# Both matrix products of a token pair by seven block products, in units of 42 matmuls

## The chip, the core and the metric

The kernel runs on one core of a Trainium2 chip. Its time is the device time of one execution, in microseconds (us). Before the change the median of three executions is 830.62 us (828.80 to 830.89).

## The reference

Attention with a sliding window of 64 positions feeds an MLP mixer: a product over tokens, then one over channels. There are 8 batches of 576 tokens, so 4608 tokens of 512 channels. All is float32. The part that the change touches is the last two lines, the channel products with 1536 hidden units:

```python
attn_out = _attn_ref(q, k, v)                    # softmax over a window of 64
x = attn_out.transpose(0, 2, 1, 3).reshape(B, S, H * D)
xt = x.transpose(0, 2, 1)
h = np.maximum(xt @ w_tok1, 0.0) @ w_tok2
u = x + h.transpose(0, 2, 1)
h2 = np.maximum(u @ w_ch1, 0.0) @ w_ch2
return u + h2
```

## The kernel before

Every float32 operand of a product is held as a high part and a low part (type float32r), and a product is three matmuls: high x high, low x high, high x low. A function `split` makes the two parts: ScalarE copies the high part (L101), another engine subtracts it from the source for the low part (L104). For hidden values `relu_split` does it with a rectifier on ScalarE (L614) and one VectorE instruction for the low part (L615).

The first 324 us compute attention and the token products and store `u` to DRAM as nine chunks of 512 tokens; they overlap with the channel products of chunk 0. Then come the channel products of chunks 1 to 8. All tiles are 128 partitions x 512 columns; the 1536 hidden units are 12 tiles, the 512 channels are 4.

*Plain chunks (0, 1, 2).* `gemm1` adds 12 matmuls into a PSUM bank for each of 12 hidden tiles, and `gemm2` makes 4 output tiles out of the 12 hidden ones, half of them at a time in chunks 1 and 2. Beside chunk 1, `weight_steps` forms sums of the blocks of `w_ch1` in float32, splits them and stores them to DRAM (`w1s`), three hidden tiles wide (384 columns), one step for each hidden tile; `quarters` are the blocks of weights that need no sum and are stored whole at the end of chunk 0.

*Pairs (chunks 3+4, 5+6, 7+8).* Two chunks of tokens and two halves of channels and of hidden units make a product of 2 x 2 blocks. `pair_f` does the first product for a hidden block `f` (6 per pair) by seven block products of 6 matmuls each, in the order of `PRODUCTS`. They go into four PSUM banks P, Q, R, S, and three products accumulate on top of an earlier one. Sums of the banks are made by VectorE in SBUF tiles `x1`, `x2`, `x3` (L853 to L865), and each of the four block results goes through `relu_split`. Its operands are combinations of the inputs (`sums`, `sum4`, `prep`), made for a whole pair beforehand by VectorE and ScalarE. After every two hidden blocks, 8 output tiles are made by plain `gemm2` calls of 12 matmuls each, with all of `w_ch2` in SBUF (`w2hi`, `w2lo`), and `add_out` (L645) adds each to the running sum `uf`.

*Order.* Each engine executes its instructions in the order of the program text; SyncE (SP) issues the loads and stores from one queue. `load_w1` fetches the block weights of a hidden block into one of three slots of the old `w1` buffers, three blocks ahead. Eight PSUM banks alternate between a hidden block and the next (`BANKS`).

## Time and profile before

| | before |
|---|---|
| median of 3 executions | 830.62 us (828.80 to 830.89) |
| span of the profiled execution | 827.4 us |
| instructions | 15250 |
| TensorE (PE) busy | 814.4 us, 98%, 5860 matmuls |
| VectorE (DVE) busy | 511.1 us, 62% |
| ScalarE (ACT) busy | 336.6 us, 41% |
| GpSimd (POOL) busy | 106.5 us, 13% |
| DMA moved | 136.51 MB, mean 165 GB/s |

The profiled execution has no time of its own beside its span; the span is 3.2 us below the median of the runs, and that distance is carried along. The page gives an average over stages of very different kinds: 324 us of attention and token products, two plain chunks, three pairs. It is read by cutting the span into these stages, and in each of them by looking for the engine that never waits. An engine's matmul rate can be read from the chain of waits, where a run of matmuls without a wait between them stands as one row. The core's 16 DMA engines share the loads and stores; SPq is the queue that SP issues to.

### The profile page before, as it was taken

The page shows a single profiled execution, that of the slowest core. Times are in us where ns is not written, and L with a number is a line of the kernel's source. Part 1 is how long each engine was busy: PE and PEld are TensorE (multiplying, and loading weights), DVE is VectorE, ACT ScalarE, POOL GpSimd, SP SyncE. Part 2 cuts the span into 40 slices and gives each one's busy share as a digit, 9 for nine tenths or more (in the row PEclk, how much of TensorE's full clock was granted, in tenths as well). Part 3 has the DMA queues.
Part 4 walks back from the last instruction along what each step waited for, and adds up shares of the span by engine and source line. Part 5 has one row for each costly group of instructions (what it writes and reads, how often), then busy time and mean ns, then how long its engine had stood idle before and what let it go on. Part 6 is the DMA issues. An engine that isn't in the chain of part 4 may idle for free.

```text
span 827.4 us, 15250 instructions
## 1 busy us (share of the span) xinstructions
PE 814.4 (98%) x5860; PEld 676.9 (82%) x5860; DVE 511.1 (62%) x1365; ACT 336.6 (41%) x1014; POOL 106.5 (13%) x117
## 2 busy tenths in 40 slices
PE   8989999999999999999999999999999999999998
PEld 6758888888889878888888888878888878888886
DVE  5987899799773993773444535277625277525352
ACT  6988989888864530331221202032202033202020
POOL 3632534444330000000000000000000000000000
PEclk9999999999999999999999999999999999999999
DMA  9847778777645629634506443334433234432002
GB/s 354 284 148 243 237 243 291 231 228 276 193 132 174 193 65 273 185 96 136 182 1 237 143 180 111 118 111 171 170 159 135 95 131 167 176 137 90 1 1 101
DMA packets 69672, 136.51 MB, mean 165 GB/s; under 512 B 7008, under 2 KB 39264, under 8 KB 67680
## 3 DMA queue, kind: packets, MB, share of 16 engines
q1 hardware_dynamic: 67488, 133.71, 47.4%
q10 hardware_dynamic: 2112, 1.84, 0.7%
q8 instruction: 46, 0.75, 0.4%
q14 instruction: 26, 0.21, 0.1%
HBM read 104.66 MB, written 30.87 MB: 164 GB/s over the span
## 4 chain that ended last, share of the span: by engine, by line
PE 84%; DVE 8%; ACT 4%; issue 2%; DMA 1%; POOL 0%; POOLq 0%; DVEq 0%; SPq 0%; ACTq 0%
PE gp L847 19%; PE op L635 11%; PE gp L627 8%; PE h L364 5%; PE up L412 5%; PE op_4a L635 4%; PE op_2b L635 4%; PE op_2a L635 4%; PE op_0b L635 4%; PE op_0a L635 4%; PE op_4b L635 4%; PE xp L316 4%; PE s L274 3%; PE pp L304 3%; PE up L405 2%; ACT e L297 2%
## 5 line engine op out<-in xcount | busy, mean ns | idle before, releaser
L847 PE MATMUL gp<-m,w1hi 128*128 128x512 f32 x504 | 155.3, 390 | 0.7 <-DVE x L855 0.7
L297 ACT ACTIVATE e<-e,nm 128x128 f32<-128x128 f32 x288 | 112.2, 397 | 6.5 <-DVE nm L289 6.3
L847 PEld LDWEIGHTS gp<-m,w1hi 128*128 128x128 f32 x504 | 94.5, 188 | 21.0 <-DVE x L855 1.5
L847 PE MATMUL gp<-m,w1lo 128*128 128x512 f32 x252 | 98.0, 389 | 0.0
L614 ACT ACTIVATE ghi<-x 128x512 fp32r<-128x512 f32 x54 | 34.1, 632 | 119.9 <-DVE x L857 68.3
L289 DVE CUSTOM_DVE_ANT_0 e<-s,mask 128x128 f32<-128x128 f32 x288 | 65.3, 285 | 10.6 <-PE s L274 10.5
L851 ACT COPY x<-gp 128x512 f32<-128x512 f32 x18 | 10.4, 578 | 143.3 <-PE gp L847 143.3
L615 DVE SCALAR_TENSOR_TENSOR glo<-x,ghi 128x512 fp32r<-128x512 f32 x54 | 37.4, 692 | 38.1 <-ACT ghi L614 38.1
L614 ACT ACTIVATE ghi<-gp 128x512 fp32r<-128x512 f32 x50 | 29.9, 597 | 70.0 <-PE gp L627 70.0
L627 PE MATMUL gp<-uhi,w1lo 128*128 128x512 f32 x144 | 56.0, 389 | 0.0
L627 PE MATMUL gp<-ulo,w1hi 128*128 128x512 f32 x144 | 56.0, 389 | 0.0
L627 PE MATMUL gp<-uhi,w1hi 128*128 128x512 f32 x144 | 56.0, 389 | 0.0
L297 ACT ACTIVATION_READ_ACCUMULATOR e<-e,nm 128x1 f32 x288 | 55.9, 194 | 0.0
L847 PEld LDWEIGHTS gp<-m,w1lo 128*128 128x128 f32 x252 | 47.3, 188 | 9.9
L615 DVE SCALAR_TENSOR_TENSOR glo<-gp,ghi 128x512 fp32r<-128x512 f32 x50 | 34.4, 688 | 25.4 <-ACT ghi L614 25.3
L635 PE MATMUL op<-glo,w2hi 128*128 128x512 f32 x128 | 49.8, 389 | 0.0
L635 PE MATMUL op<-ghi,w2hi 128*128 128x512 f32 x128 | 49.8, 389 | 0.0
L635 PE MATMUL op<-ghi,w2lo 128*128 128x512 f32 x128 | 49.8, 389 | 0.0
L316 PEld LDWEIGHTS xp<-v,pt 128*64 128x64 f32 x1152 | 36.6, 138 | 12.9 <-ACT e L297 9.4
L104 POOL TENSOR_TENSOR xlo<-x,xhi 128x512 fp32r<-128x512 f32 x32 | 41.6, 1300 | 43.6 <-ACT xhi L101 42.9
L304 PE MATMUL pp<-ident,e 128*128 128x128 f32 x288 | 45.4, 282 | 1.5
L274 PE MATMUL s<-k,q 64*64 64x128 f32 x1152 | 41.8, 277 | 2.6 <-DMA k<-kh 0.9
(161 smaller groups left out, 1827.9 us busy)
## 6 DMA issues: line engine op xcount, KB each, us to landing
v<-vh SPq DMA_DIRECT2D x36, 512.0 KB, 4.4
w1hi<-w1s SPq DMA_DIRECT2D x18, 896.0 KB, 4.7
w1lo<-w1s SPq DMA_DIRECT2D x18, 896.0 KB, 6.5
raw<-wc SPq DMA_DIRECT2D x32, 384.0 KB, 4.6
q<-qh SPq DMA_DIRECT2D x36, 256.0 KB, 4.7
k<-kh SPq DMA_DIRECT2D x7, 1280.0 KB, 7.7
out<-uf SPq DMA_DIRECT2D x35, 256.0 KB, 2.7
uf<-u_dram SPq DMA_DIRECT2D x8, 1024.0 KB, 9.1
```

What stands on the lines that cost most here:

```text
L104: eng_lo.tensor_sub(lo, src, hi.bitcast(F32))
L274: nc.tensor.matmul(so, qt[r, j, half], kbs[b][r, n:n + 2, j], start=True, stop=True)
L289: nc.vector.tensor_tensor_reduce(out=e[:, h], in0=s[:, h], in1=mk, scale=-scale, scalar=MAX_F32, op0=ALU.add, op1=ALU.min, accum_out=nm[:, ...
L297: nc.scalar.activation(e[:, h], e[:, h], AF.Exp, bias=nm[:, g:g + 1], scale=-1.0, accum_out=sm[:, g:g + 1])
L304: nc.tensor.transpose(pp[:, h], e[:, h], ident)
L316: nc.tensor.matmul(xp[half * BLK:(half + 1) * BLK, h], pts[h % 2][:, h // 2, half * BLK:(half + 1) * BLK], vt[:, half, h], start=True, sto ...
L364: nc.tensor.matmul(h_ps[b][tt], w[:, o + tt * P:o + (tt + 1) * P], x, start=first and n == 0, stop=last and n == len(combos) - 1)
L614: nc.scalar.activation(hi, src, AF.Relu)
L615: nc.vector.scalar_tensor_tensor(out=lo, in0=src, scalar=0.0, in1=hi.bitcast(F32), op0=ALU.max, op1=ALU.subtract)
L627: nc.tensor.matmul(gp, w[:, w1_at(ft, ct)], x[:, ct], start=(k == 0), stop=(k == 3 * NCT - 1))
L635: nc.tensor.matmul(op, w[:, ct, ft], x[:, cols], start=(first and k == 0), stop=(last and k == 3 * len(gs) - 1), skip_group_check=not (fir ...
L847: nc.tensor.matmul(b, w[:, at], c[:, h, t], start=(n < 4 and k == 0), stop=(k == 5), skip_group_check=True)
```

## The change

- The pair's second product is done by seven block products too. A pair is now 12 units of 42 matmuls: in each of three groups two units of the first product (hidden blocks 2g and 2g+1), then two of the second (output tiles ct = 0 and 1, in the order of `ORDER2`).
- The operands of the second product are the hidden blocks and sums of them. `first_product` makes them: the adds of banks write into banks Q, S and R; `raw_block`/`raw_low` rectify and split a block on ScalarE and VectorE, `positive` makes the sums of rectified blocks on VectorE, and `sum_block` splits these with the high part on ScalarE and the low part on GpSimd. In `PRODUCTS`, m3 now stands ahead of m4.
- `second_product` accumulates into four banks and adds them to the running sums of the outputs; `u2` holds a sum that two outputs of every row share, and is added to them in the last group.
- The block weights of both products come in one stream: `load_unit` fetches one unit's weights (1.8 MB) into one of three slots, three units ahead.
- `weight_steps` now runs for both weight matrices, 256 columns wide, with three store buffers instead of four: two steps per hidden tile in the first eight of chunk 1, one per hidden tile and output tile after that, to the end of chunk 2. The blocks of `w_ch2` that need no sum are stored in 12 transfers of 384 KB during chunk 1 (`quarters2`).
- The input combinations of the next pair are made in the last group, their low parts and sums mostly on GpSimd.

The diff, cut to its core:

```diff
-PRODUCTS = ("m1", "m6", "m7", "m5", "m2", "m4", "m3")
+PRODUCTS = ("m1", "m6", "m7", "m5", "m2", "m3", "m4")
...
-        def weight_steps():
...
+        def weight_steps(name, whi, wlo, part, store, swap):
+            for n in range(2 * NG):
...
                 def keep(m, x):
-                    hi, lo = (pw.tile([P, CW], F32R, name=f"w{k}_{m}_{n}", tag=f"w{k}", bufs=4) for k in ("hi", "lo"))
+                    hi, lo = (pw.tile([P, WW], F32R, name=f"{name}{k}_{m}_{n}", tag=f"w{k}", bufs=3) for k in ("hi", "lo"))
                     split(nc.scalar, nc.vector, hi, lo, x)
                     for k, t in enumerate((hi, lo)):
-                        store_w1(m, k, f0, ct, t)
+                        store(m, k, f0, ct, t)
...
+        def load_unit(n):
+            if n < (NCHUNK - N_PLAIN) // 2 * UNITS:
                 o = n % NSLOT * SLOT
+                g, i = divmod(n % UNITS, 4)
                 for k, w in enumerate((w1hi, w1lo)):
+                    src = w1s[k][:, 2 * g + i] if i < 2 else w2s[k][:, g, i - 2]
+                    nc.sync.dma_start(w[:, o:o + SLOT].bitcast(F32), src.rearrange("p m t c -> p (m t c)"))
...
                     gemm1(j, ft, u, g[-1])
+                    for _ in range(2 if j == 1 and ft < 8 else 1):
+                        next(steps, None)
                     if j == 1:
-                        next(steps, None)
+                        m, k, t, o = quarters2[ft]
+                        store_w2(m, k, 0, t, (w2hf, w2lf)[k][:, o:o + NH * P])
...
-        def pair_f(q, f):
...
+        def positive(out, x, y):
+            nc.vector.scalar_tensor_tensor(out=out, in0=x, scalar=0.0, in1=y, op0=ALU.max, op1=ALU.subtract)
+        def first_product(n, q, f, after):
...
+            def raw_block(m, x):
+                nc.scalar.activation(gc[m, i][0], x, AF.Relu)
+            def raw_low(m, x):
+                positive(gc[m, i][1], x, gc[m, i][0].bitcast(F32))
+            def sum_block(m, x):
+                split(nc.scalar, nc.gpsimd, *gc[m, i], x)
...
                 elif m == "m5":
-                    nc.vector.tensor_add(x3, b, x2)
-                    done(1, f + NH, x3)
+                    nc.vector.tensor_add(qq, ss, x2)
+                    raw_block("m3", qq)
+                    raw_low("m3", qq)
                 elif m == "m2":
-                    done(0, f, b)
+                    nc.scalar.activation(g11, pp, AF.Relu)
+                    raw_block("m1", pp)
+                    raw_low("m1", pp)
+                elif m == "m3":
+                    nc.vector.tensor_add(ss, ss, x1)
+                    positive(t1, ss, g11)
+                    sum_block("m5", t1)
+                    positive(t2, qq, t1)
+                    sum_block("m6", t2)
+                    positive(t3, pp, t2)
+                    sum_block("m7", t3)
                 else:
-                    nc.vector.tensor_add(x1, b, x1)
-                    done(1, f, x1)
+                    nc.vector.tensor_add(rr, rr, x1)
+                    raw_block("m2", rr)
+                    positive(t4, rr, t2)
+                    raw_low("m2", rr)
+                    sum_block("m4", t4)
+                after(m)
...
+        ORDER2 = (("m1", 0), ("m1", 1), ("m6", 0), ("m7", 0), ("m5", 0), ("m5", 1), ("m6", 1), ("m7", 1),
+                  ("m2", 0), ("m2", 1), ("m3", 0), ("m3", 1), ("m4", 0), ("m4", 1))
+        def second_product(n, q, g, ct, ufs, u2, after):
...
+            for m, i in ORDER2:
+                o = n % NSLOT * SLOT + (PRODUCTS.index(m) * 2 + i) * P
+                hi, lo = gc[m, i]
+                bank = b[INTO[m]]
...
+                    for y, (w, x) in enumerate(((w1hi, hi), (w1hi, lo), (w1lo, hi))):
+                        nc.tensor.matmul(bank[:, cols], w[:, o:o + P], x[:, cols],
+                                         start=(i == 0 and y == 0 and m in ("m1", "m6", "m7", "m5")),
+                                         stop=(i == 1 and y == 2), skip_group_check=True)
...
+            for g in range(NG):
+                final = more and g == NG - 1
+                for i in range(2):
+                    first_product(n, q, 2 * g + i, last_first if final and i == 1 else nothing)
+                    load_unit(n + NSLOT)
...
+                for ct in range(2):
+                    second_product(n, q, g, ct, ufs, u2[ct],
+                                   (last_second0, last_second1)[ct] if final else nothing)
+                    load_unit(n + NSLOT)
```

How the order of instructions moves is shown at four places. A row names line, operation, output <- inputs and size.

VectorE before, hidden block 2 of the first pair. The `gp` are the banks P, Q, R, S (0 to 3), the `x` are the SBUF sums, `ghi`/`glo` the parts of a hidden tile:

```order
L853 TENSOR_TENSOR x_0_2_6345<-gp_2_1_6342,x_0_2_6345 128x512
L855 TENSOR_TENSOR x_0_2_6346<-gp_2_2_6343,x_0_2_6345 128x512
L857 TENSOR_TENSOR x_0_2_6347<-gp_2_3_6344,x_0_2_6346 128x512
L615 SCALAR_TENSOR_TENSOR glo_8_6377<-x_0_2_6347,ghi_8_6376 128x512
L615 SCALAR_TENSOR_TENSOR glo_2_6387<-gp_2_0_6341,ghi_2_6386 128x512
L862 TENSOR_TENSOR x_0_2_6346<-gp_2_2_6343,x_0_2_6345 128x512
L615 SCALAR_TENSOR_TENSOR glo_8_6398<-x_0_2_6346,ghi_8_6397 128x512
L865 TENSOR_TENSOR x_0_2_6345<-gp_2_3_6344,x_0_2_6345 128x512
L615 SCALAR_TENSOR_TENSOR glo_2_6409<-x_0_2_6345,ghi_2_6408 128x512
```

VectorE after, the same hidden block (`g12t`, `g22t` and the `g` are sums of blocks in SBUF; m1 to m3 are operands of the second product):

```order
L897 TENSOR_TENSOR x_0_2_6710<-gp_2_1_6693,x_0_2_6710 128x512
L899 TENSOR_TENSOR x_0_2_6711<-gp_2_2_6694,x_0_2_6710 128x512
L901 TENSOR_TENSOR gp_2_1_6693<-gp_2_3_6695,x_0_2_6711 128x512
L860 SCALAR_TENSOR_TENSOR m3lo_2_6707<-gp_2_1_6693,m3hi_2_6706 128x512
L860 SCALAR_TENSOR_TENSOR m1lo_2_6697<-gp_2_0_6692,m1hi_2_6696 128x512
L909 TENSOR_TENSOR gp_2_3_6695<-gp_2_3_6695,x_0_2_6710 128x512
L860 SCALAR_TENSOR_TENSOR g12t_2_6713<-gp_2_3_6695,g_0_2_6712 128x512
L860 SCALAR_TENSOR_TENSOR g22t_2_6714<-gp_2_1_6693,g12t_2_6713 128x512
L860 SCALAR_TENSOR_TENSOR g_0_2_6715<-gp_2_0_6692,g22t_2_6714 128x512
L917 TENSOR_TENSOR gp_2_2_6694<-gp_2_2_6694,x_0_2_6710 128x512
L860 SCALAR_TENSOR_TENSOR g_0_2_6716<-gp_2_2_6694,g22t_2_6714 128x512
L860 SCALAR_TENSOR_TENSOR m2lo_2_6705<-gp_2_2_6694,m2hi_2_6704 128x512
```

Nine instructions have become twelve; three of them write into banks, and four low parts of the second product are made elsewhere. ScalarE after, from the same block into the next one:

```order
L905 ACTIVATE g_0_2_6712<-gp_2_0_6692 128x512
L876 ACTIVATE m1hi_2_6696<-gp_2_0_6692 128x512
L105 CAST m5hi_2_6702<-g12t_2_6713 128x512
L105 CAST m6hi_2_6698<-g22t_2_6714 128x512
L105 CAST m7hi_2_6700<-g_0_2_6715 128x512
L876 ACTIVATE m2hi_2_6704<-gp_2_2_6694 128x512
L105 CAST m4hi_2_6708<-g_0_2_6716 128x512
L895 COPY x_0_3_6804<-gp_3_0_6786 128x512
```

The last row is the copy of the next block's first product, which used to follow a rectifier and now follows the high part of m4. TensorE after, ten rows into the second product of the first group (`op` are its banks):

```order
L949 MATMUL op_1_0_3_6903<-m5hi_3_6796,w1hi 128x512
L949 MATMUL op_1_0_3_6903<-m5lo_3_6797,w1hi 128x512
L949 MATMUL op_1_0_3_6903<-m5hi_3_6796,w1lo 128x512
L949 MATMUL op_1_0_1_6901<-m6hi_3_6792,w1hi 128x512
L949 MATMUL op_1_0_1_6901<-m6lo_3_6793,w1hi 128x512
L949 MATMUL op_1_0_1_6901<-m6hi_3_6792,w1lo 128x512
L949 MATMUL op_1_0_2_6902<-m7hi_3_6794,w1hi 128x512
L949 MATMUL op_1_0_2_6902<-m7lo_3_6795,w1hi 128x512
L949 MATMUL op_1_0_2_6902<-m7hi_3_6794,w1lo 128x512
```

The sums of the second hidden block (number 3), low parts from GpSimd, are read from the 16th matmul of the second product on. SP in chunk 1 after, from its second hidden tile on:

```order
L660 DMA w1s_69<-uhi_m_0_5131 128x2x128
L660 DMA w1s_70<-ulo_m_0_5132 128x2x128
L666 DMA w2s_71<-w2hi 384x1x256
L660 DMA w1s_69<-uhi_m_0_5157 128x2x128
L660 DMA w1s_70<-ulo_m_0_5158 128x2x128
L660 DMA w1s_69<-uhi_m_0_5163 128x2x128
L660 DMA w1s_70<-ulo_m_0_5164 128x2x128
```

Where there were only stores of three hidden tiles' width (192 KB), there are more and narrower ones (128 KB) and stores of 384 KB between them.

## Rows read from the trace of the kernel before

**Rows 1.** The page: span, and busy time of each engine.

```profile
span 827.4 us, 15250 instructions
...
PE 814.4 (98%) x5860; PEld 676.9 (82%) x5860; DVE 511.1 (62%) x1365; ACT 336.6 (41%) x1014; POOL 106.5 (13%) x117
```

**Rows 2.** Windows (us, engines' busy time, clock, DMA): chunks 1, 2, the first pair.

```profile
324.18:389.46 65.28, 65.28 (x289) 54.05 (x289) 40.28 (x72) 16.77 (x32) 0.00 (x0) 1.00 0.51 149
389.46:454.74 65.28, 65.28 (x289) 54.05 (x289) 28.53 (x44) 14.42 (x26) 0.00 (x0) 1.00 0.39 138
454.74:577.77 123.03, 122.69 (x541) 101.28 (x541) 64.42 (x99) 25.82 (x44) 0.00 (x0) 1.00 0.38 137
```

**Rows 3.** Chain of waits at the first pair's start: start, us, what.

```profile
454.74 19.04 PE gp L847 x84
```

**Rows 4.** Timeline of one hidden block: start, us, engine, line, operation [idle before <-releaser].

```profile
495.38 0.61 PE L847 MATMUL gp<-m,w1hi 128*128 128x512 f32 x2
...
496.74 0.61 PE L847 MATMUL gp<-m,w1hi 128*128 128x512 f32 x2
...
496.99 0.59 ACT L851 COPY x<-gp 128x512 f32<-128x512 f32 x1 [21.06 <-PE gp L847]
...
501.02 0.69 DVE L857 TENSOR_TENSOR x<-gp,x 128x512 f32<-128x512 f32 x1 [0.67 <-PE gp L847]
...
501.74 0.63 ACT L614 ACTIVATE ghi<-x 128x512 fp32r<-128x512 f32 x1 [4.16 <-DVE x L857]
...
502.41 0.69 DVE L615 SCALAR_TENSOR_TENSOR glo<-x,ghi 128x512 fp32r<-128x512 f32 x1 [0.70 <-ACT ghi L614]
...
503.01 0.69 DVE L615 SCALAR_TENSOR_TENSOR glo<-gp,ghi 128x512 fp32r<-128x512 f32 x1
```

**Rows 5.** Timeline at the end of the first pair, VectorE and ScalarE.

```profile
548.53 0.68 DVE L745 TENSOR_TENSOR t<-r,r 128x512 f32<-128x512 f32 x1
...
549.25 0.69 DVE L747 TENSOR_TENSOR r<-r,r 128x512 f32<-128x512 f32 x1
...
554.72 0.60 ACT L101 CAST m<-t 128x512 fp32r<-128x512 f32 x1
...
555.23 0.59 ACT L614 ACTIVATE ghi<-gp 128x512 fp32r<-128x512 f32 x1
```

**Rows 6.** The same timeline, where TensorE waits for VectorE.

```profile
552.26 0.69 DVE L855 TENSOR_TENSOR x<-gp,x 128x512 f32<-128x512 f32 x1
...
553.00 0.74 PE L847 MATMUL gp<-m,w1hi 128*128 128x512 f32 x2 [0.34 <-DVE x L855]
```

**Rows 7.** Timeline in the attention stage, ScalarE and GpSimd.

```profile
83.89 0.62 ACT L101 CAST xhi<-x 128x512 fp32r<-128x512 f32 x1
...
84.59 1.28 POOL L104 TENSOR_TENSOR xlo<-x,xhi 128x512 fp32r<-128x512 f32 x1 [0.35 <-ACT xhi L101]
...
97.92 1.28 POOL L345 TENSOR_TENSOR xhi<-x,xhi 64x512 fp32r<-64x512 f32 x1 [0.35 <-ACT xhi L344]
99.28 1.30 POOL L345 TENSOR_TENSOR xlo<-x,xlo 64x512 fp32r<-64x512 f32 x1
```

**Rows 8.** Groups of VectorE in the pairs: busy us, mean ns | idle before.

```profile
L853 DVE TENSOR_TENSOR x<-gp,x 128x512 f32<-128x512 f32 x18 | 12.4, 691 | 17.4 <-PE gp L847 17.0
...
L747 DVE TENSOR_TENSOR r<-r,r 128x512 f32<-128x512 f32 x4 | 2.8, 692 | 3.1 <-DMA r<-u_dram 3.0
```

**Rows 9.** Chunk 1: ScalarE's wait for a buffer; windows before and early in it.

```profile
345.85 0.52 ACT L101 CAST whi_m<-wa 128x384 fp32r<-128x384 f32 x1 [2.93 <-DMA w1s<-wlo_m]
...
315.00:320.00 5.00, 5.00 (x24) 4.14 (x23) 0.69 (x1) 0.00 (x0) 0.00 (x0) 1.00 1.01 299
325.00:330.00 5.00, 5.00 (x24) 4.14 (x23) 1.62 (x3) 0.88 (x2) 0.00 (x0) 1.00 0.84 249
```

**Rows 10.** DMA issues of the first pair: count, KB each, median us to landing.

```profile
w1lo<-w1s SPq DMA_DIRECT2D x6, 896.0 KB, 6.4
...
uf<-u_dram SPq DMA_DIRECT2D x2, 1024.0 KB, 9.4
```

More of the change, by code (lines that the diff above doesn't have):

```diff
@@ L60 @@
 SLOT, NSLOT = NPROD * 2 * P, 3
+NG = NH // 2
+UNITS = 4 * NG
+WW = 2 * P
 NEG = -2.0 ** 33
@@ L96, in mixer_kernel @@
     w1s = [dram.tile([P, NH, NPROD, 2, P], F32, name=f"w1s{k}") for k in range(2)]
+    w2s = [dram.tile([P, NG, 2, NPROD, 2, P], F32, name=f"w2s{k}") for k in range(2)]
     u_dram = [dram.tile([P, NCT, CHUNK], F32, name=f"u_dram{j}") for j in range(NCHUNK)]
@@ L556, in mixer_kernel @@
     with ExitStack() as bctx:
-        pb = bctx.enter_context(tc.tile_pool(name="pb", bufs=1, reuse_waits="tile"))
+        p6 = bctx.enter_context(tc.tile_pool(name="p6", bufs=1, side="right", reuse_waits="tile"))
+        plain = ExitStack()
+        pb = plain.enter_context(tc.tile_pool(name="pb", bufs=1, reuse_waits="tile"))
         w2hi = pb.tile([P, NCT, NFT, P], F32R, name="w2hi")
@@ L808, in mixer_kernel @@
                     add_out(j, u[0], ct, op, half == 1)
-                    if j == 1:
-                        next(steps, None)
+                    next(steps, None)
                     if last and half == 1 and ct == 1:
@@ L815, in mixer_kernel @@
                             prep(0, m, 0)
+        assert next(steps, None) is None
+        tctx.close()
+        plain.close()
+        pg = bctx.enter_context(tc.tile_pool(name="pg", bufs=1, reuse_waits="tile"))
+        pools[1] = pg
         BANKS = ((("s", 2), ("s", 2), ("pt", 2), ("pt", 2)), (("av", 1), ("up", 1), ("h", 2), ("h", 2)))
         def banks(name, odd):
-            return [ps.tile([P, CHUNK], F32, name=f"{name}_{n}", tag=tag, bufs=bufs)
-                    for n, (tag, bufs) in enumerate(BANKS[odd])]
@@ L823, in pair_f @@
-        def pair_f(q, f):
-            bank = dict(zip("PQRS", banks(f"gp{q}_{f}", f % 2)))
-            into = {"m1": "P", "m6": "Q", "m7": "R", "m5": "S", "m2": "P", "m4": "R", "m3": "S"}
-            x1, x2, x3 = (px[0].tile([P, CHUNK], F32, name=f"x{n}_{q}_{f}", tag=f"x{n}", bufs=2 if n == 1 else 1)
-                          for n in (1, 2, 3))
-            o = (q * NH + f) % NSLOT * SLOT
-            g = {}
-            def done(c, ft, src):
-                g[c, ft] = new_g(f"{pairs[q][c]}_{ft}")
-                relu_split(*g[c, ft], src)
-            more = f == NH - 1 and q + 1 < len(pairs)
-            if more:
-                sums()
-            for n, m in enumerate(PRODUCTS):
-                b, c = bank[into[m]], comb[q, m]
-                order = (1, 0) if q == 0 and m in ("m4", "m3") else (0, 1)
-                k = 0
-                for t in order:
-                    at = slice(o + (n * 2 + t) * P, o + (n * 2 + t + 1) * P)
-                    for w, h in ((w1hi, 0), (w1hi, 1), (w1lo, 0)):
-                        nc.tensor.matmul(b, w[:, at], c[:, h, t], start=(n < 4 and k == 0), stop=(k == 5),
-                                         skip_group_check=True)
-                        k += 1
@@ L873, in mixer_kernel, with nothing, last_first, last_second0 @@
+        n = 0
         for q, (ja, jb) in enumerate(pairs):
+            more = q + 1 < len(pairs)
+            u2 = [pg.tile([P, CHUNK], F32, name=f"u2_{q}_{ct}", tag=f"u2{ct}", bufs=1) for ct in range(2)]
             ufs = []
-            final = q == len(pairs) - 1
-            for f0 in range(0, NH, 2):
-                gs = []
-                for f in (f0, f0 + 1):
-                    if f == NH - 2 and not final:
-                        load_raw(q + 1, 0)
-                    gs.append(pair_f(q, f))
-                    load_w1(q * NH + f + NSLOT)
-                    if f == 1:
+            def nothing(m):
+                pass
+            def last_first(m):
+                if m in ("m1", "m6"):
+                    for t in range(2):
+                        prep(q + 1, m, t, t, nc.gpsimd)
+            def last_second0(m):
+                if m in ("m1", "m6", "m7"):
+                    for t in range(2):
+                        prep(q + 1, {"m1": "m7", "m6": "m5", "m7": "m2"}[m], t, t, nc.gpsimd)
+            def last_second1(m):
+                if m == "m1":
+                    for t in range(2):
+                        sum4(t, nc.gpsimd)
+                if m in ("m6", "m7"):
+                    for t in range(2):
+                        prep(q + 1, {"m6": "m3", "m7": "m4"}[m], t, t)
+            for g in range(NG):
[3 more added lines that the diff above has]
+                    load_unit(n + NSLOT)
+                    if n % UNITS == 0:
```

200 lines of the change are left out of this document (126 added, 74 removed).

## The prediction

> **What bounds the kernel now.** I read the profile in four steps. First the page's busy times: TensorE is busy for 814.4 of a span of 827.4 us [rows 1]. Then the busy times by stage: in the two plain chunks that the change touches (chunks 1 and 2) and in the first pair, to which the other two are alike, TensorE has no idle time worth the name, VectorE is busy for 40.28 and 28.53 us of 65.28 in the chunks and for 64.42 of 123.03 in the pair, and GpSimd does nothing at all [rows 2]. Then the chain of waits: through the pairs it is one TensorE piece after another, 84 matmuls in 19.04 us, which is 0.2267 us for a matmul of 512 columns [rows 3]. So from 324 us on, time is the number of such matmuls, as long as the other engines stay ahead. Last, the single instructions of a pair, to learn how long a hand-over from one engine to the next takes, because the change lives on those.
>
> **What the change takes away.** Of a pair, the first product is 6 x 42 = 252 matmuls in both versions. The second is 8 outputs x 12 hidden tiles x 3 = 288 before and 6 x 42 = 252 now. So 36 matmuls go per pair, 108 in all: 108 x 0.2267 = **-24.5 us**. All of it lies on the path that sets the end.
>
> **What it puts beside TensorE in a pair.** A unit is 42 matmuls, 9.52 us; one block product is 6 matmuls, 1.36 us. In a first-product unit VectorE now issues 12 instructions (order section: 9 before), ScalarE 9 (5 before), GpSimd 4 (none before). Back to back a VectorE instruction of 128x512 takes 0.60 us (502.41 to 503.01) [rows 4], so 12 make 7.2 of 9.52 us: it fits by sum. Whether it fits by order has to be followed, because VectorE and ScalarE now hand results to each other several times in one unit. The steps are these:
>
> - end of a block product on TensorE to the first reader: 0.25 us (496.74 to 496.99), 0.20 on VectorE (the fourth product ends at 500.82, four times 1.36 behind the 495.38 at which the unit begins, and VectorE starts at 501.02) [rows 4];
> - VectorE start to a ScalarE start that needs it: 0.72 (501.02 to 501.74) [rows 4]; to its own next dependent instruction also 0.72 (548.53 to 549.25) [rows 5];
> - ScalarE start to VectorE: 0.67 (501.74 to 502.41) [rows 4]; ScalarE back to back 0.51 (554.72 to 555.23) [rows 5];
> - ScalarE start to GpSimd 0.70 (83.89 to 84.59); GpSimd back to back 1.36 (97.92 to 99.28) [rows 7];
> - VectorE start to a TensorE that waits for it: 0.74 (552.26 to 553.00), and the first two matmuls after the wait take 0.74 instead of 0.61, so 0.13 more [rows 6].
>
> Count from the start of the first unit of a group (two first-product units, then two second-product units). Unit 1, VectorE: the add into bank Q at 5.64; ScalarE's m3hi at 6.36; m3lo 7.03; m1lo 8.23 (behind g11 and m1hi on ScalarE, 7.05 and 7.56); the add into S 8.83; the three block sums 9.55, 10.27, 10.99; the add into R 11.59; m2hi on ScalarE 12.31; t4 12.98; m2lo 13.58; and m4hi on ScalarE 13.70. Behind m4hi on ScalarE's queue stands the copy of the *next* unit's m1, which could have run at 11.1 and now runs at 14.21. VectorE's chain of the second unit therefore starts at 14.88, and its add into Q, which reads bank S, at 16.32. TensorE wants to go on accumulating into S at 16.32 (9.52 + 5 x 1.36), gets it at 17.06, and loses 0.74 + 0.13 = **0.87 us**. From there: m3 ends at 18.55, add into S at 19.33, block sums 20.05, 20.77, 21.49; their high parts on ScalarE 20.77, 21.49, 22.21; their low parts on GpSimd, one after the other, 21.47, 22.83, 24.19. The third is done at 25.55. The second product starts at 19.91, and its 23rd matmul needs that part at 24.90: 0.65 + 0.13 = **0.78 us**. The low parts of the first two are there in time (22.83 against 23.54; 24.19 against 24.22, so with nothing to spare). In the two second-product units VectorE has 7 adds of 0.60 in 9.52 us and catches up. Sum 1.65 us a group, nine groups: **+14.9 us**.
>
> **The operation that no row shows** is a VectorE write *into* a PSUM bank (the adds into Q, S and R). Call its surcharge p. Reading PSUM costs nothing: the add from a bank is 691 ns, the one from SBUF alone 692 [rows 8]. From below I take -0.03 (ScalarE is faster from PSUM: a rectifier out of a bank 0.59, out of SBUF 0.63 [rows 4, 5]), from above a second pass over the tile, +0.60 [rows 4]. I take p = 0, the VectorE rows being the nearest. Four such writes stand in the chain before the first stall and a fifth in the one before the second, so a group's loss is 1.65 + 5p, up to about 4.6 at p = 0.60. The trace has no difference between a PSUM and an SBUF source. [...]
>
> **Chunk 1.** Here the change adds, per hidden tile of the first eight, two steps of weight sums instead of one, and 12 stores of 384 KB. Up to the sixth hidden tile, 16.3 us, SP issues 24 stores of 128 KB, 6 of 384 KB and 1 MB of chunk 2's input: 6.5 MB. The queue moved 299 GB/s when it was full of such stores [rows 9], so they need 21.9 us. What waits is ScalarE: a high part needs its buffer (three instead of four) back from a store. Before, it already waited 2.93 us for one, without harm, in a stretch where nothing queued behind it mattered [rows 9]. Now the rectifier of the sixth tile stands behind such a wait. The stores ahead of it (10 of 128 KB, 3 of 384 KB, 2.5 MB) are 8.4 us after the queue has drained chunk 0's stores, which it still works on at 325 to 330 [rows 9]: about 331 + 8.4 + 2 = 341.4 (the 2 for the way of the last store itself: a load of 896 KB takes 6.4 us [rows 10], 3.1 of them by its bytes at 299 GB/s), and the rectifier about 1 us later. TensorE needs that tile 15 matmuls after the last first-layer matmul, 340.5 + 3.4 = 343.9. It fits by a little over 1 us, against an uncertainty larger than that: I take **+1.5 us**, bounds 0 and +6. Chunk 2 has one step per tile beside what it had; VectorE is less than half busy there [rows 2]: **+0.5**, bounds 0 and 2.
>
> **Smaller edits.** From pair to pair, the combinations of the next pair's inputs move mostly to GpSimd, whose queue holds 4 low parts (5.4 us) per unit and is free in the second product; they delay the last group's low parts by some 0.3 us: **+0.6** for two hand-overs. Before, VectorE made them and TensorE waited for it at the end of the first pair, 123.03 [rows 2] against 540 x 0.2267 = 122.4 us, and I take it likewise in the second: **-1.2** at most when that goes, of which I count **-0.7**, twice the 0.34 idle that a row proves [rows 6]. Weights: one unit is 1.8 MB and its slot is released two units, 19 us, before it is needed; the second half of such a load landed 6.4 us after its issue [rows 10]. At nothing. The pair's two inputs of 1 MB queue behind that load and landed 9.4 us after issue [rows 10], about 20.5 us into the pair; VectorE first adds to them at 24. At nothing, with 3 us of cover. The last matmuls are halved in both versions: nothing.
>
> **Sum.** 827.4 - 24.5 + 14.9 + 1.5 + 0.5 + 0.6 - 0.7 = 819.7 us of span. The median of the runs, 830.62, lies 3.2 above the profiled span; with that, **823 us**.
>
> **Rivals.**
> *The hand-overs cost less than I add up.* The two stalls of a group rest on margins of tenths: with VectorE's dependent step at 0.60 instead of 0.72 the eight such steps before the first stall save about 0.9 us and it vanishes. For: before, a similar chain of five hand-overs never stopped TensorE outside the hand-over to the next pair [rows 3]. Against: the copy that stands behind m4hi is in the order, not in the durations. At 0 to 0.5 us a group: 808 to 813.
> *Slower: PSUM writes are dear.* Place: the adds into Q, S and R. [...] With p = 0.30 a group loses 3.1 us, 28 in all, 836; with 0.60 849. It turns the gain into a loss of 0.3% once a group loses more than 2.8 us, p = 0.23. Nothing in the trace speaks for it but that it shows no such write.
> *The stores of chunk 1 hold up the rectifiers.* +6 in place of +1.5 (with 1.5 in chunk 2): 828 to 830. For: the queue has to move 6.5 MB in 16.3 us and can move 4.9.
> *The stream of weights is late,* 36 loads of 1.8 MB, 193 GB/s beside everything else. At the 149 GB/s of chunk 1 [rows 2] a unit would last 12 us and the kernel would end near 915. Against: the 299 GB/s above. Here the change would not do what it says.
>
> **Chances.** Forecast 0.52 (its own range 817 to 829), cheap hand-overs 0.13, dear PSUM writes 0.20, chunk 1's stores 0.11, late weights 0.04. The range 812 to 837 leaves out half of the cheap case, the dear end of the PSUM case and the late weights. No change to this measurement is 0.3%, 828.1 to 833.1. Faster: 0.49 of the forecast's 0.52, 0.13, and a third of the chunk-1 case: 0.66. The same: 0.13. Slower: 0.21, nearly all of it the PSUM case.
>
> **What would show it.** Right: TensorE's matmul count down by 108; in each group one wait of the first product's sixth block for VectorE's add into Q, in the second unit only, near 0.8 us, and one wait of the second product for GpSimd near 0.7; VectorE near 82 us busy per pair, GpSimd near 40. Wrong: adds into PSUM longer than 0.72 us; waits in both units; waits for ScalarE in chunk 1 longer than 3 us in sum; TensorE waiting for a load.

## The result, and the profile after

The changed kernel takes 831.18 us (median of 16 executions, 830.33 to 833.02), the kernel before 828.90 us (16, 828.42 to 831.67). The ratio is 1.0026, with a 95% interval of 1.0017 to 1.0036. The forecast was 823 us, a gain of 7.6 from the three executions it started from (830.62); measured is a loss of 2.3 us against the 16. The page of after, lines 1 and 3, which answer to [rows 1]:

```profile
span 829.1 us, 15813 instructions
...
PE 800.3 (97%) x5749; PEld 654.7 (79%) x5749; DVE 603.1 (73%) x1545; ACT 389.4 (47%) x1124; POOL 246.4 (30%) x225
```

111 matmuls fewer are in the trace: the 108 of the forecast, and 3 because halving the end of the last output makes 6 more matmuls before and 3 more after. TensorE is busy for 14 us less, and the span is 1.7 us longer: TensorE now waits. For what, the view of waits of after says (TensorE from 320 us on; total us, times, longest):

```profile
PE gp L892 <- DVE gp L901: 5.6, 9, 0.7
PE op L949 <- DVE uf L939: 3.6, 5, 1.1
PE gp L892 <- ACT x L895: 3.3, 1, 3.3
PE op L949 <- POOL m7lo L108: 2.2, 9, 0.3
PE op L641 <- ACT ghi L620: 1.0, 1, 1.0
PE op L641 <- DVE glo L621: 0.6, 3, 0.2
```

Before, the same view had three waits in all, 1.2 us. The windows of after tell where the time is lost (first two windows of the length that chunks 1 and 2 had before, though chunk 1 now lasts from 323.66 to 390.72 and chunk 2 to 457.05; then the second group of the first pair and its last; columns as in [rows 2]). The last group holds the hand-over, the passage from one pair to the next:

```profile
324.20:389.50 65.30, 64.11 (x282) 52.52 (x281) 46.60 (x105) 19.23 (x43) 0.00 (x0) 1.00 0.73 226
389.50:454.80 65.30, 64.89 (x286) 53.02 (x285) 47.43 (x97) 20.05 (x43) 0.00 (x0) 1.00 0.52 173
...
501.61:541.53 39.92, 39.01 (x169) 31.27 (x169) 25.37 (x38) 10.48 (x18) 17.79 (x14) 1.00 0.65 237
541.53:583.52 41.99, 39.53 (x169) 31.11 (x169) 32.59 (x45) 17.96 (x32) 26.92 (x20) 1.00 0.59 207
```

A group is 168 matmuls, 38.09 us at the 0.2267 of [rows 3]; it takes 39.92, so 1.83 are lost, and 3.9 in a group with a hand-over. Busy time hides part of this, since the first matmuls behind a wait are longer (0.74 us for the two at 518.86, 0.62 for two without a wait). So the loss is counted from matmul start to matmul start, beyond 0.2267 each: 1.8 us in chunk 1, 1.0 in chunk 2, 5.2 in the first unit of the first pair, 15.0 in nine groups, 4.2 in the two hand-overs, 0.9 in the last matmuls; 28.1 us in all, against the 24.5 that the change had to give and about 2 that were lost in the same way before.

**The first pair's start.** The chain of waits of after, where [rows 3] had 84 matmuls in one piece:

```profile
452.12 12.49 DMA w2s<-dhi_m
...
465.30 0.59 ACT x L895
...
465.93 2.94 PE gp L892 x6
```

ScalarE and SP there, and the windows around it:

```profile
464.99 0.40 ACT L105 CAST dhi_m<-wdd 128x256 fp32r<-128x256 f32 x1 [6.39 <-DMA w2s<-dhi_m]
465.30 0.58 ACT L895 COPY x<-gp 128x512 f32<-128x512 f32 x1
...
446.72 1.74 SPq L764 DMA_DIRECT2D r<-u_dram  x4
...
449.98 0.38 SPq L755 DMA_DIRECT2D w1lo<-w2s  x1
...
452.12 0.56 SPq L666 DMA_DIRECT2D w2s<-dhi_m  x1
...
455.00:464.00 9.00, 7.65 (x34) 6.01 (x32) 4.87 (x10) 1.73 (x4) 0.00 (x0) 1.00 1.02 406
464.00:470.00 6.00, 4.07 (x11) 3.25 (x12) 3.20 (x5) 2.57 (x5) 0.00 (x0) 0.72 0.47 163
```

The last weight step's high part needs a buffer whose store was issued at 452.12, behind 1 MB of pair inputs and two units of weights (3.6 MB); the DMA engines are full (a busy share of 1.02) at 406 GB/s, and the store takes 12.49 us. ScalarE stands for 6.39 us, and the first unit's copy of bank P stands behind it. TensorE waits 3.27 us, and for the next 3.4 us its granted clock is 0.50 (0.72 on the mean of the second window).

**A group's second unit** (timeline of after, the same instructions as in [rows 4]):

```profile
515.38 0.62 ACT L105 CAST m4hi<-g 128x512 fp32r<-128x512 f32 x1 [0.83 <-DVE g L860]
515.90 0.58 ACT L895 COPY x<-gp 128x512 f32<-128x512 f32 x1
...
516.52 0.69 DVE L897 TENSOR_TENSOR x<-gp,x 128x512 f32<-128x512 f32 x1 [0.58 <-ACT x L895]
517.31 0.69 DVE L899 TENSOR_TENSOR x<-gp,x 128x512 f32<-128x512 f32 x1
518.11 0.70 DVE L901 TENSOR_TENSOR gp<-gp,x 128x512 f32<-128x512 f32 x1
...
516.54 0.72 PE L892 MATMUL gp<-m,w1hi 128*128 128x512 f32 x2
...
518.86 0.74 PE L892 MATMUL gp<-m,w1hi 128*128 128x512 f32 x2 [0.67 <-DVE gp L901]
...
527.14 0.50 PE L949 MATMUL op<-m7lo,w1hi 128*128 128x512 f32 x1 [0.24 <-POOL m7lo L108]
```

These are the two waits that were forecast, at their places. The row at 516.54 was not: TensorE itself starts m2 only when the copy has ended (515.90 + 0.58), because m2 accumulates into the bank that is copied.

**Chunk 1** (VectorE, ScalarE and TensorE at the wait in its middle):

```profile
343.06 0.42 DVE L727 TENSOR_TENSOR wsu<-wsu,wau 128x256 f32<-128x256 f32 x1
343.56 0.40 ACT L105 CAST uhi_m<-wsu 128x256 fp32r<-128x256 f32 x1 [1.93 <-DVE wsu L727]
343.87 0.59 ACT L620 ACTIVATE ghi<-gp 128x512 fp32r<-128x512 f32 x1
...
344.51 0.50 PE L641 MATMUL op<-ghi,w2hi 128*128 128x512 f32 x1 [0.97 <-ACT ghi L620]
```

The rectifier of the sixth hidden tile stands on ScalarE behind a weight step's high part, and that waits for VectorE's sum, not for a store.

**A hand-over** (VectorE, GpSimd, TensorE at the end of the first pair; the last two rows are the same VectorE adds in the last pair, where GpSimd has no such work):

```profile
568.51 1.56 DVE L939 TENSOR_TENSOR uf<-u,uf 128x512 f32<-128x512 f32 x1
570.17 0.69 DVE L939 TENSOR_TENSOR uf<-op,uf 128x512 f32<-128x512 f32 x1
...
568.22 2.99 POOL L108 TENSOR_TENSOR m<-r,m 128x512 fp32r<-128x512 f32 x2
...
570.92 0.50 PE L949 MATMUL op<-m4hi,w1hi 128*128 128x512 f32 x1 [0.41 <-DVE uf L939]
...
811.43 0.69 DVE L939 TENSOR_TENSOR uf<-u,uf 128x512 f32<-128x512 f32 x1
812.22 0.69 DVE L939 TENSOR_TENSOR uf<-op,uf 128x512 f32<-128x512 f32 x1
```

An add within SBUF takes 1.56 us beside GpSimd and 0.69 without it; the add that frees bank R for m4 stands behind it.

### The profile page after: what moved, and what is told of

Read it like the earlier page. It is cut to its first block, busy times and chain, and to the rows that moved or that the text cites. A ratio compares the mean times of both kernels' runs of the same rounds, so it can differ in the third digit from the quotient of the medians.

```text
span 829.1 us, 15813 instructions
## 1 busy us (share of the span) xinstructions
PE 800.3 (97%) x5749; PEld 654.7 (79%) x5749; DVE 603.1 (73%) x1545; ACT 389.4 (47%) x1124; POOL 246.4 (30%) x225
## 5 line engine op out<-in xcount | busy, mean ns | idle before, releaser
L892 PE MATMUL gp<-m,w1hi 128*128 128x512 f32 x504 | 158.4, 396 | 8.8 <-DVE gp L901 5.6
L108 POOL TENSOR_TENSOR m5lo<-g12t,m5hi 128x512 fp32r<-128x512 f32 x18 | 23.4, 1299 | 418.9 <-ACT m5hi L105 418.9
L939 DVE TENSOR_TENSOR uf<-op,uf 128x512 f32<-128x512 f32 (+1 forms) x91 | 61.0, 681 | 43.6 <-PE op L949 42.9
L217 POOL TENSOR_TENSOR w<-r,c 128x384 f32<-128x384 f32 (+1 forms) x28 | 27.6, 986 | 70.2 <-DVE r L215 67.8
L416 PE MATMUL up<-t2hi,hhi 128*128 128x320 f32 (+1 forms) x128 | 43.1, 337 | 0.6 <-ACT t2hi L105 0.6
```

What stands on the lines that cost most here:

```text
L108: eng_lo.tensor_sub(lo, src, hi.bitcast(F32))
L416: nc.tensor.matmul(up[:, :n], hx[:, cs], w[:, tt * S + s0:tt * S + s0 + n], start=False, stop=(k == 6), skip_group_check=True)
L892: nc.tensor.matmul(b[INTO[m]], w[:, at], c[:, h, t], start=(k < 4 and z == y == 0), stop=(z == 1 and y == 2), skip_group_check=True)
L939: nc.vector.tensor_add(x, y, x)
```

## The experiments

Ratios are to the kernel before; the changed kernel stands at 1.0026, so 0.001 is 0.83 us.

**1. The pair's third load, later.**

```diff
                     load_raw(0, 0)
                     load_unit(1)
-                    load_unit(2)
...
         assert next(steps, None) is None
+        load_unit(2)
```

> The changed kernel with one load moved: the weights of the pair's third unit (1.8 MB) are issued behind the last stores of weight sums, not ahead of them. Theory (the first unit of the first pair stands behind ScalarE, which waits for a store buffer, whose store is queued behind 5 MB of loads): the wait of 3.3 us and the half clock after it go, 5.2 us in all, so about 826 us, ratio to the kernel before 0.9963 (0.995 to 0.9985). Rival (the wait is for the inputs of the pair or for late weights of units 0 and 1, which stay where they are): nothing changes, 1.0026; and if unit 2's weights then come late, TensorE waits for a load at the third unit.

826.11 us, ratio 0.9963 [0.9951, 0.9975]: 5.2 us less. The high part's wait on ScalarE is now 2.40 us and ends at 459.0, so the copy runs at 459.3, before TensorE needs bank P again; TensorE has no wait there, and the clock shows no drop before the end (its mean in the profiled execution is 1.0, and 0.997 in the changed kernel). The wait and the lower clock go together, as the theory says, and the time is the forecast one.

**2. VectorE's order in the last group.**

```diff
                     add(u2, bank)
-                    if final:
-                        add(c22, u2)
                 elif m == "m7":
                     add(c22, bank)
+                    if final:
+                        add(c22, u2)
...
-                if m in ("m6", "m7"):
+                if m in ("m2", "m3"):
                     for t in range(2):
-                        prep(q + 1, {"m6": "m3", "m7": "m4"}[m], t, t)
+                        prep(q + 1, {"m2": "m3", "m3": "m4"}[m], t, t)
```

> The changed kernel with VectorE's order in the last group of a pair changed: the add that frees bank R for m4 goes ahead of the add within SBUF, and the two splits of m3 and m4 for the next pair go behind the adds of m2 and m3. GpSimd's work is the same. Theory (TensorE waits for bank R because VectorE executes slow SBUF adds and splits ahead of that add): both waits of a hand-over, 0.67 and 1.40 us, go, 4.1 us in the two hand-overs, ratio 0.9977 (0.9965 to 0.999). Rival (VectorE is late there because of its backlog from the first product, whatever the order): less than 1 us, 1.0015 to 1.003.

827.31 us, 0.9979 [0.9968, 0.9989], 3.9 us less. Of the five waits for `uf` only the one ahead of the last half matmuls is left, 0.5 us. Order it was; the slow adds are still there (1097 ns on the mean, 945 in the changed kernel), but nothing waits behind them.

**3. GpSimd beside VectorE's adds.** Six subtractions on GpSimd that nothing uses, in the last pair.

```diff
+            def idle_work(m):
+                if m in ("m1", "m6", "m7"):
+                    for t in range(2):
+                        r = raws[t]
+                        nc.gpsimd.tensor_sub(r["t1"], r["r12"], r["r11"])
```

> The changed kernel with six extra subtractions on GpSimd in the last group of the last pair (unit 10 of its 12), at the places where the other pairs have GpSimd's splits for the next pair; their results are used by nothing. Theory (VectorE's adds within SBUF are slowed by GpSimd working in SBUF at the same time): the adds of the shared sum to an output in that unit take 1.2 to 1.6 us instead of 0.69, and TensorE waits 0.3 to 0.7 us ahead of m4 there. Rival (the slow adds of the hand-overs have to do with the loads or the ScalarE copies of the next pair, which are absent here): 0.69 us stays, and no wait.

Its timeline (VectorE, GpSimd, TensorE):

```profile
811.03 0.68 DVE L939 TENSOR_TENSOR u<-op,u 128x512 f32<-128x512 f32 x1
811.75 1.55 DVE L939 TENSOR_TENSOR uf<-u,uf 128x512 f32<-128x512 f32 x1
...
811.43 8.91 POOL L1014 TENSOR_TENSOR t<-r,r 128x512 f32<-128x512 f32 x6
...
814.14 0.50 PE L949 MATMUL op<-m4hi,w1hi 128*128 128x512 f32 x1 [0.37 <-DVE uf L939]
```

The add that took 0.69 us takes 1.55, and TensorE waits where it did not. Adds that read a bank keep 0.67 to 0.69. This one is shown: GpSimd's subtractions slow VectorE's adds whose two inputs are both in SBUF, here from 0.69 to 1.55 us.

**4. The copy ahead.** The second unit's first block product and its copy are issued ahead of the sums behind m4.

```diff
                 else:
+                    if ahead:
+                        nxt = open_unit(n + 1, q, f + 1)
                     nc.vector.tensor_add(rr, rr, x1)
```

> The changed kernel with the first block product of a group's second unit, and ScalarE's copy of it, issued ahead of the sums behind m4 of the first unit. TensorE's order is the same; ScalarE makes the copy ahead of m2's and m4's high parts. Theory (the wait for the add into Q in the second unit comes from the copy that stands behind m4's high part): the copy is done 1.4 us or more earlier, VectorE's chain starts 0.66 us earlier, the wait of 0.97 us falls to about 0.3, and the wait for GpSimd grows by 0.1 to 0.2: 0.5 us a group, 4.5 us, ratio 0.9972 (0.996 to 0.9985). Rival (VectorE's own sum of work sets it): no change, 1.0026.

828.96 us, 1.0002 [0.9988, 1.0015]: 2.0 us less, not 4.5. VectorE in a second unit:

```profile
513.86 0.69 DVE L860 SCALAR_TENSOR_TENSOR g<-gp,g22t 128x512 f32<-128x512 f32 x1 [1.14 <-POOL m6lo L108]
514.47 0.68 DVE L860 SCALAR_TENSOR_TENSOR m2lo<-gp,m2hi 128x512 fp32r<-128x512 f32 x1
515.07 0.68 DVE L909 TENSOR_TENSOR x<-gp,x 128x512 f32<-128x512 f32 x1
```

The first add no longer waits for the copy, but it stands behind t4, and t4 starts when m2's rectifier ends (513.15 + 0.60), which the copy now precedes on ScalarE. The row names GpSimd's low part of m6 instead, which ends at about the same time; but in the changed kernel t4 began 0.3 us before the end of that part (514.65 against 513.70 + 1.29), so it does not need it. Only TensorE's own slip at m2 went; the wait for the add into Q is still 0.66. The copy's place alone was not the cause.

**5. t4 ahead of m2's rectifier.**

```diff
                     nc.vector.tensor_add(rr, rr, x1)
-                    raw_block("m2", rr)
                     positive(t4, rr, t2)
+                    raw_block("m2", rr)
```

> The changed kernel with one line moved: VectorE's sum t4, which needs only the add into R, is issued ahead of ScalarE's rectifier of m2, not behind it. In the changed kernel's trace t4 begins only when that rectifier ends, 0.73 us after VectorE is free. Theory (VectorE's queue sets when the second unit's sums can begin, and this wait is part of it): t4 starts 0.6 to 0.7 us earlier, m4's high part and the copy behind it too, the wait for the add into Q falls from 0.97 to about 0.3, the wait for GpSimd's low part of m7 stays or grows by 0.1 to 0.2: about 0.55 us a group, 5 us, ratio to the kernel before 0.9966 (0.9955 to 0.998). Rival (t4 waits for a buffer that a reader still holds, not for the rectifier's place in the order): no change, 1.0026.

829.58 us, 1.0010 [0.9999, 1.0021], 1.3 us less. t4 does start without a wait; now the rectifier waits for t4, and the copy is only a little earlier. The wait stays at 0.67, and a group loses 0.15 us less.

**6. m1's low part later.**

```diff
-                    raw_low("m1", pp)
...
                     sum_block("m7", t3)
+                    raw_low("m1", pp)
...
-        ORDER2 = (("m1", 0), ("m1", 1), ("m6", 0), ("m7", 0), ("m5", 0), ("m5", 1),
+        ORDER2 = (("m1", 0), ("m6", 0), ("m7", 0), ("m5", 0), ("m1", 1), ("m5", 1),
```

> The changed kernel with m1's low part made on VectorE behind the three sums instead of ahead of the add into S, and with the second product taking m1's second block after m5's first. Theory (VectorE's idle time of 0.48 and 0.28 us in front of m1's low part delays the sums, and with them GpSimd's low parts and the next unit): both waits of a group shrink by about 0.5 us, so the wait for m7's low part goes and the one for the add into Q halves; 1 us a group, 9 us, ratio 0.992 (0.990 to 0.996). Rival (GpSimd's three low parts, one after another, set the second wait, whatever VectorE does): the first wait alone halves, 4 us, 0.998.

833.66 us, 1.0058 [1.0042, 1.0074]: slower. The nine waits for m7's low part go, as expected, but six for the copy (0.36 from start to start) and six for the add of the second product's first sum (0.34) take their place, and the wait for Q stays at 0.83. A group loses about 0.3 us more on the mean.

**7. Chunk 1's whole-block stores in chunk 2.**

```diff
-                    if j == 1:
+                    if j == 2:
                         m, k, t, o = quarters2[ft]
```

> The changed kernel with the 12 stores of 384 KB of whole weight blocks moved from the hidden tiles of chunk 1 to those of chunk 2. Theory (the wait of 1.7 us in the middle of chunk 1 comes from store buffers whose stores queue behind these): it goes, and chunk 2 and the start of the pair lose up to 0.5 us more: ratio 1.0006 (1.000 to 1.0016). Rival (the rectifier is late because two weight steps a hidden tile are too much for ScalarE and VectorE, whatever the queue moves): 1.0026, with the same wait. If the start of the first pair gets worse (the stores now stand nearer to its loads), above 1.003.

834.69 us, 1.0063 [1.0049, 1.0077]. Chunk 1 loses what it lost (0.97 and 0.22 us at the same two matmuls); the start of the pair is worse, a wait of 4.1 us and behind it matmuls that start 0.42 to 0.51 us apart for 5.3 us, where the changed kernel had 2.7 us of them. These stores were not the cause in chunk 1.

**8. Chunk 1's double steps spread.**

```diff
-                    for _ in range(2 if j == 1 and ft < 8 else 1):
+                    for _ in range(2 if j == 1 and ft in (0, 1, 2, 3, 6, 7, 8, 9) else 1):
```

> The changed kernel with chunk 1's double weight steps at hidden tiles 0 to 3 and 6 to 9 instead of 0 to 7, so one step each at the last two tiles ahead of the second layer. Stores and their sizes are the same. Theory (the rectifier of the sixth tile stands on ScalarE behind a high part that waits for VectorE, which is behind with two steps a tile; no store is involved): the wait of 1.7 us in the middle of chunk 1 goes, ratio 1.0006 (1.000 to 1.0015). Rival (it is the stores' buffers): the wait stays, 1.0026.

833.80 us, 1.0067 [1.0047, 1.0088]. The wait in the middle of chunk 1 is gone, and two such waits stand at the end of its second half, where VectorE also splits the next chunk's input. The loss follows the double steps; the kernel as a whole is no better, because chunk 1 now loses 3.7 us, 1.9 more than in the changed kernel; in the profiled execution the start of the first pair loses 1.1 us more as well.

**9. Edits 1, 2, 5 and 6 together.**

> The changed kernel with four edits together: unit 2's load later, the order of the last group, t4 ahead of m2's rectifier, and m1's low part later. If the losses are independent: 5.2 + 4.1 us of the start and the hand-overs, and 1.2 to 1.6 us of the 1.6 us that a group loses, 11 to 14 us: about 810 us (807 to 815), ratio 0.977 (0.974 to 0.983). If VectorE's or GpSimd's sum of work sets the group (the waits only move): 816 to 821, 0.985 to 0.99.

823.11 us, 0.9928 [0.9914, 0.9942]. That is slower than both forecasts. The hand-overs' waits go, and so does the start's wait for the copy, though a wait for Q of 0.7 us appears in that first unit. The group loses 1.8 us on the mean, against 1.7 in the changed kernel. TensorE and VectorE in a second unit:

```profile
512.17 0.69 DVE L897 TENSOR_TENSOR x<-gp,x 128x512 f32<-128x512 f32 x1 [0.30 <-ACT x L895]
512.97 0.69 DVE L899 TENSOR_TENSOR x<-gp,x 128x512 f32<-128x512 f32 x1
513.76 0.70 DVE L901 TENSOR_TENSOR gp<-gp,x 128x512 f32<-128x512 f32 x1
...
512.19 0.73 PE L892 MATMUL gp<-m,w1hi 128*128 128x512 f32 x2
...
514.52 0.73 PE L892 MATMUL gp<-m,w1hi 128*128 128x512 f32 x2 [0.66 <-DVE gp L901]
```

Here the size of the wait can be read. The copy (511.55 + 0.59) releases TensorE's m2 and VectorE's chain at the same moment, 512.17 and 512.19. From there TensorE needs one block product, 1.36 us plus the 0.13 of a first matmul, and VectorE three adds that follow each other, 2.3 us. Where the copy releases both, as here, in the changed kernel and in run 5, an earlier copy makes both earlier and leaves the wait as it is. In run 4 the copy came 2 us earlier in its group, but the first add, behind t4 and m2's low part, started only 0.25 us earlier, and the wait was the same.

**10. The second unit's first add ahead too.**

```diff
                     positive(t4, rr, t2)
+                    if ahead:
+                        block(n + 1, q, 1, nxt[0])
+                        nc.vector.tensor_add(nxt[1], nxt[0]["Q"], nxt[1])
                     raw_block("m2", rr)
...
-                    raw_low("m2", rr)
                     sum_block("m4", t4)
+                    if ahead:
+                        raw_low("m2", rr)
+                    else:
+                        nxt = lambda: raw_low("m2", rr)
```

> The changed kernel with the second unit's first block product, its copy, its second block product and VectorE's first add issued ahead of m2's parts of the first unit, t4 ahead of m2's rectifier, and the second unit's m2 low part behind the first add of the second product. Theory (the second unit's wait is the time of ScalarE's copy and three adds of 0.8 us that follow each other, against one block product of 1.36 us; it vanishes only when both the copy and the first add come early): the add into Q starts 1 us earlier against TensorE, the wait of 0.83 us and the slip of 0.2 us before it go, the one for GpSimd's m7 stays at 0.5: 1.0 to 1.2 us a group, 10 us, ratio to the kernel before 0.991 (0.989 to 0.994). Rival (three adds of 0.8 us against 1.36 us are too long by themselves, wherever they start): the wait stays, 1.000 to 1.002.

The nine waits for Q are gone, and a group loses 0.5 us where it lost 1.7. But the time is 834.39 us, 1.0080 [1.0051, 1.0109], its nine executions between 825.0 and 842.2 with mean clocks from 0.994 to 0.983; the profiled one is the fastest. In the profile the hand-overs grew: TensorE comes earlier to the same slow adds and waits 1.8 us in each. Windows behind the second of them:

```profile
698.00:700.00 2.00, 0.79 (x3) 0.70 (x4) 2.00 (x4) 0.06 (x1) 0.00 (x0) 0.96 0.54 226
700.00:702.00 2.00, 2.00 (x6) 1.52 (x6) 2.00 (x4) 0.00 (x0) 0.00 (x0) 0.50 0.35 131
702.00:704.00 2.00, 2.00 (x8) 1.57 (x7) 1.36 (x3) 0.13 (x1) 0.00 (x0) 0.69 0.50 184
```

The clock fell there for 3.4 us (0.96, 0.50 and 0.69 on the means of the three windows), as at the start (0.93, 0.50 and 0.72 from 466 to 472). At a clock of 0.50, a mean of 0.988 is some 20 us at the lower level in an execution, against 10 in the profiled one (0.994). By an estimate from these means the clock accounts for about 5 of the 9 us between the profiled execution and the median; where the drops of the others stand, and what the rest is, was not seen.

**11. All edits together,** with edit 6 and the spread steps.

> All edits together: unit 2's load later, the order of the last group, the first add of the second unit ahead, m1's low part later, the spread steps of chunk 1. If the losses are independent: 5.2 + 4.1 + 1.7 us and 1.3 to 1.6 us for each of nine groups go, 23 to 25 us of 27: about 807 us (805 to 811), ratio 0.974 (0.971 to 0.979). If a group keeps half of its loss because VectorE or GpSimd is full: 814, 0.982.

815.79 us, 0.9844 [0.9817, 0.9870]. That is slower than both forecasts. Start, groups and hand-overs lose 4.0 us in all; chunk 1 loses 5.3, with a drop of the clock behind its waits (matmuls 0.42 to 0.43 us apart from 383.15 to 386.14).

**12. The double steps behind the layer.**

```diff
-                    for _ in range(2 if j == 1 and ft in (0, 1, 2, 3, 6, 7, 8, 9) else 1):
+                    for _ in range(2 if j == 1 and ft < 4 else 1):
...
                     add_out(j, u[0], ct, op, half == 1)
-                    next(steps, None)
+                    for _ in range(2 if j == 1 and half == 0 else 1):
+                        next(steps, None)
```

> As the run with all edits together, but chunk 1's double weight steps stand at hidden tiles 0 to 3 and behind the four output tiles of its first half, where VectorE has one add in 4 us and no rectifier is due. Theory (a step delays a rectifier only where VectorE is behind ahead of a second layer): the 5.3 us that chunk 1 lost in that run fall to under 1 us, no drop of the clock is left but at the end, and the time is 810 us (808 to 812), ratio to the kernel before 0.977 (0.975 to 0.980). Rival (the steps are late anywhere in chunk 1, by the stores' buffers): 1.7 us or more stay, above 812.

808.74 us, 0.9756 [0.9743, 0.9769]: 2.4% faster than the kernel before, 22 us below the changed kernel. Its waits (as above), and windows of a chunk's length, most of it chunk 1, and of a group:

```profile
PE op L972 <- POOL m7lo L108: 0.6, 2, 0.3
PE op L972 <- DVE uf L962: 0.5, 1, 0.5
PE op L641 <- DVE glo L621: 0.4, 2, 0.2
...
324.20:389.50 65.30, 65.30 (x289) 53.80 (x288) 46.31 (x104) 19.12 (x43) 0.00 (x0) 1.00 0.77 232
496.11:534.39 38.28, 38.28 (x169) 31.38 (x168) 25.29 (x38) 10.28 (x18) 17.83 (x14) 1.00 0.68 247
```

The same stores move in the same chunk, and chunk 1 loses 0.2 us. Chunk 2 still loses the 1.0 that it lost in every run.

## Why the prediction was wrong

By its own steps, forecast and measured (us of span):

| step | forecast | measured |
|---|---|---|
| 108 matmuls | -24.5 | -24.5 by count and rate |
| nine groups | +14.9 | +15.0 |
| chunk 1 | +1.5 | +1.8 |
| chunk 2 | +0.5 | +1.0 |
| start of the first pair | 0 | +5.2 |
| hand-overs, less the old waits | -0.1 | +2.9 |
| all | -7.7 | +1.7 |

The measured terms add up to 1.4. To the 1.7 of the spans come 0.5 behind the last matmul and 0.1 in the last matmuls, less 0.4 by which chunk 1 begins earlier (all rounded). The forecast span, 819.7, is 9.4 too low; the forecast median is 8.2 too low, because the median lies 2.1 above the span and not 3.2.

- **The matmuls and the groups** were right, engines and places too: one wait for the add into Q in the second unit only, one for GpSimd. That the sum fits to 0.1 us is in part luck: the two waits (0.87 and 0.78 forecast; 0.97 and 0.52, with a slip of 0.2 at m2) err in opposite directions, and the first group of a pair loses 1.2 to 1.5 us where the others lose 1.8. GpSimd's low parts follow each other at 1.25 us (512.45, 513.70, 514.95 in the timeline of after), not at the 1.36 taken. The reason given for the first wait, the copy behind m4's high part, was half of it: TensorE hangs on the same copy, which the count left out, and runs 5 and 9 show that the stall is the length of three adds against one block product. Only run 10, which takes one of the three out of that stretch, ends it.
- **A write into a bank** was the open price. The adds into Q, S and R take 700, 690 and 690 ns on the mean, the one into SBUF 692: p = 0, as taken, and the rival of dear writes falls.
- **The step that failed is "Chunk 2 has one step per tile beside what it had; VectorE is less than half busy there: +0.5", with the weights "At nothing".** The steps were priced by VectorE's busy time. Chunk 2 itself lost 1.0. But the steps run to the end of chunk 2, and their stores go through the one queue on which the first pair's loads had just been put. The prediction followed exactly such a wait (ScalarE, a store buffer, a full queue) through chunk 1, and did not ask at which other place a load stands ahead of a store: the start of the first pair, taken at nothing, cost 5.2 of the 9.4 us. This is the largest part of the miss, and run 1 shows it.
- **The hand-overs** are the second part: put at -0.1, they cost 2.9. GpSimd's low parts were priced by GpSimd's own time (near 40 us a pair; it was busy for 54.8 in the first), and the last group's extra adds of the shared sums were not counted ("VectorE has 7 adds of 0.60": in the last group there are 10, and four splits in a hand-over). Run 2 shows the order, run 3 the slowing: the add within SBUF takes 0.69 us alone and 1.55 beside GpSimd's subtractions, and adds with a bank as a source keep 0.67 to 0.69. What in the two engines makes it so is not shown.
- **Chunk 1** had the right size for the wrong reason. The prediction let the rectifier wait for a store; run 7 moved the stores of whole blocks and nothing changed. It stands behind a high part that waits 1.93 us for VectorE, which is behind with two steps a tile; run 8 moved the wait, run 12 removed it.
- **Late weights** never occurred: the units' loads landed 4.5 to 6.5 us after issue on the median (7.6 to 12.7 at the start of the first pair), and TensorE waited for none.

## What to carry to other kernels

Here a wait cost whatever was queued behind it on the same engine (6.39 us on ScalarE for a store held up a copy, and TensorE waited 3.27 for that): for every instruction that waits for a DMA, look at what the queue holds ahead of that DMA at that very time, at the borders between stages above all. When a stall keeps its size through edits that should shorten it, look for an event that releases both sides at once; then the length of the chain from it is what counts. And price work given to GpSimd by what it does to VectorE's instructions beside it (0.69 us became 1.55 in run 3), not by GpSimd's own time alone.

## What the runs showed of the hardware

- TensorE's granted clock fell to 0.50 for 3.41 us after a wait of 3.27 us (the changed kernel), and its matmuls started 0.42 to 0.51 us apart from 465.93 to 468.65, for 2.72 us, against 0.2267 at the full clock. In run 7, after 4.09, they did so for 5.28 us. The longer stretch does not go with the longer wait: in run 2 it was 2.72 us after 4.35, in run 8 5.29 after 3.42; what decides it is not shown. In the profile of run 10 it fell after one of its two waits of 1.8 us, and not after the other; it did not fall after the waits of 1.13 and 1.10 us in the hand-overs of the changed kernel (1.00 from 570 to 584 and from 691 to 705). At the start of the first pair, the wait of 3.27 us cost 5.2 with the half clock behind it.
- A VectorE add that needs the result of the one ahead of it starts 0.72 us after it in [rows 5], but 0.79 to 0.80 in the chain of a second unit (516.52, 517.31, 518.11), although the busy time is the same (0.69). The trace of after shows the difference: in each step of 0.80 a separate semaphore wait stands in VectorE's queue between the two (an EVENT_SEMAPHORE of 0.02 us at 517.25, 0.07 ahead of the add at 517.31), which waits for VectorE's own count, while the add itself waits for TensorE's. In the first unit of a pair, where the sum waits for VectorE's count alone and carries that wait itself, the step is 0.72 to 0.73 from bank sources too (471.35 to 472.07). The forecast took 0.72 for all of them.
- Six subtractions on GpSimd took VectorE's add within SBUF from 0.69 to 1.55 us (run 3); adds with a bank as a source kept 0.67 to 0.69, and adds that write into a bank took 0.69 to 0.70.
